# Four heads by 32 keys in a score tile, value rows through a DRAM tensor, and halved first projections, in a two-layer attention kernel

## The chip, the cores and the metric

The kernel runs on one core of a Trainium2 chip. The metric is the device time of one execution in microseconds (us), as the median of several runs. A profile of one execution gives the rest. The engines are TensorE (PE, with PEld for its weight loads), VectorE (DVE), ScalarE (ACT), GpSimd (POOL) and SyncE (SP); each works through its own queue in order. In this kernel SP computes nothing: it issues nearly all of the DMAs, the DMA transposes among them.

## What is computed

Four blocks follow each other on x (2048 tokens of 512 numbers): A, B, A, B, each added to x after a layer norm. Both have 32 heads of 16 dimensions. A is causal softmax attention inside four segments of 512 tokens, mixed by a gate with a linear-attention memory of the earlier segments. B is linear attention over all tokens, with softmax feature maps. The gate g depends on the head alone.

```python
# A, per segment s of 512 tokens (the rest of the head's state is M and z)
logits = einsum('bhqd,bhkd->bhqk', qs, ks) * scale + mask      # causal
a_dot  = einsum('bhqk,bhkd->bhqd', softmax(logits), vs)
a_mem  = (phi(qs) @ M) / (phi(qs) @ z + 1e-06)
o      = g * a_mem + (1 - g) * a_dot
M, z   = M + phi(ks).T @ vs,  z + sum(phi(ks))
...
# B
phi_q, phi_k = [softmax(p), softmax(-p)] of q @ w_phi and k @ w_phi
o = (phi_q @ (phi_k.T @ v)) / (phi_q @ sum(phi_k) + 1e-06)
```

## The kernel before

**Order.** The program is first recorded as a graph of operations, with the tiles that they read, write and open. Then `place` (L157) reads a packed table, `ORDER`: it gives the place of each operation in one sequence, its engine where there is a choice (an eviction of a PSUM tile can go to ACT or to DVE), and the buffer of each tile. Nothing is planned at run time: each engine works off its operations in the table's order and waits on semaphores for what an operation needs. An operation that waits holds up all behind it on its engine, on SP too. Pools hold the buffers: four PSUM tiles of 128x1024 (`pD`), three buffers of masked keys (`pQ`, class KM), 22 general buffers of 1024 columns (`p2`, where the exponentials PT lie), two of values (`pV`, VT), two of swapped values (`pW`, VS), two of PE and three of PF for the exponentials at the diagonal. (The class PE, tile `pE`, is not the engine PE.)

**Projections.** `a_proj` (L695) makes keys, queries and values of a segment. For each pair of head groups (a group is 8 heads, 128 rows) K and Q come out of TensorE with tokens along the columns (`KQ`, matmuls of 64 rows and 512 columns, two row halves side by side, `pair` at L330), are evicted to `KT` and `QT`, and `kmask` (L666) spreads the keys: four DVE instructions per pair multiply KT by a column mask, so that in KM a block of 128 columns holds 64 keys of one head beside 64 keys of another, with zeros in the rows of the other heads. In the first segment K and Q of one group share one PSUM tile, so that a tile waits for all 512 tokens.

**Scores.** `a_att` (L819) treats two query tiles of 128 at once (256 queries, `i0` is 0 or 2) for each of four groups g. A score tile in PSUM is 128 rows (two heads by 64 keys) by 1024 columns (two row halves, two blocks of 64 keys, 256 queries). For key tiles ahead of the diagonal (`j < i0`) all of it is needed: label S, four tiles in a group when i0 is 2, none when it is 0, one ACT exponential of 1024 columns each. At the diagonal a group has three tiles: two of 896 columns (label Sf, exponential to `pF`) and one of 768 (label Sd, to `pE`): the causal edge is cut in steps of 64 queries. The triangle itself is added in PSUM by two matmuls of a tile, of a constant (`two64`) with the mask `tri`.

**Values.** The exponentials are the weights of the PV matmuls (label PV, `pvmm` at L871), 64 rows (64 keys of one head) by 128 queries; 17 value columns (16 and a one that sums the row) are the moving side, written twice, the second time to columns nobody reads, so that a matmul has 34 columns. Values are evicted to VT with tokens as rows. A head whose exponentials lie in the other half of the rows needs its values there too: two DMAs of a segment (`vsw`, L760, both from SP) copy half of VT to VS with the row halves swapped, inside SBUF. Half of the PV matmuls read VT, half VS.

Per segment follow the memory products, the output projection, a layer norm and B's keys (`b_keys`); after four segments B's queries (`b_query`), and then layer two. Where the text says (L, s), it means layer L, segment s, from 0.

## Time and profile before

| what | value |
|---|---|
| time, median of 3 runs | 466.94 us (466.38 to 467.51) |
| profiled execution, span from the first to the last instruction | 466.4 us |
| mean granted TensorE clock | 0.996 |
| instructions | 25392 |

The runs' time holds some half a microsecond that lies outside the profiled span (466.94 against 466.4). The page gives for each engine its busy time, the time per 40th of the span, the chain of work that ended last (followed back from the last instruction, each step to what released it), and groups of instructions by source line, engine and operation, with the mean time of one. In a group, "xcount | busy, mean" are the count, the union of their times in us and the mean of one in ns. Two things to know: many operations are recorded through helpers, so L351 is any ACT instruction, L326 and L341 any matmul, L360 a DVE eviction; and an ACT or PE instruction's time holds some 0.1 us and more of pipeline beyond the moment at which the next one starts, so that the time from one start to the next, as the chain shows it, is the smaller and is what a queue pays.

### The profile page before, as it was taken

Reading aid. Unit: us, or ns where it says so; the run is one execution under the profiler, and the core shown is the slowest. Engines: PE = TensorE matmul, PEld = TensorE weight load, DVE = VectorE, ACT = ScalarE, POOL = GpSimd, SP = SyncE. Lnnn points to the kernel's source line nnn. Section 1 sums busy time; section 2 is a strip of 40 time slices with the busy share of each in tenths; the row PEclk is TensorE's granted clock in tenths of the full one; section 3 lists DMA queues with packets and bytes.
Section 4 is the critical chain, followed back from the end, with each engine's and each line's share of the span. In section 5 each row is a group of like instructions: output and inputs, shape, how many; then the busy total and the mean of one; then the engine's idle time right before and its main releaser. Section 6 shows DMA issues by size and latency. Waiting matters only on the chain.

```text
span 466.4 us, 25392 instructions
## 1 busy us (share of the span) xinstructions
PE 444.9 (95%) x11765; PEld 296.2 (64%) x11765; DVE 410.1 (88%) x761; ACT 426.3 (91%) x556; POOL 55.6 (12%) x139
## 2 busy tenths in 40 slices
PE   8999999899999999998899999999999999999897
PEld 4457566666766686655546677566767676667554
DVE  5998889799779978986899999899988896999897
ACT  5899999899999999688999999999999999877992
POOL 2433011010011001100311221010100020110000
PEclk9999999999999999998999999999999999999999
DMA  8965653703212121200134564441233004110255
GB/s 260 191 132 123 87 88 57 74 5 71 51 26 49 21 42 28 38 7 4 32 62 84 77 96 75 70 73 37 47 41 59 17 15 60 27 25 1 38 94 181
DMA packets 87755, 29.96 MB, mean 64 GB/s; under 512 B 74322, under 2 KB 87650, under 8 KB 87650
## 3 DMA queue, kind: packets, MB, share of 16 engines
q1 hardware_dynamic: 86818, 27.81, 33.7%
q8 instruction: 92, 1.51, 1.4%
q10 hardware_dynamic: 800, 0.52, 0.4%
q0 software_dynamic: 32, 0.02, 0.2%
q14 instruction: 13, 0.11, 0.1%
HBM read 6.31 MB, written 2.10 MB: 18 GB/s over the span
## 4 chain that ended last, share of the span: by engine, by line
PE 59%; ACT 30%; DVE 6%; DMA 2%; POOL 1%; issue 1%; DVEq 0%; ACTq 0%
PE D L341 38%; PE D L326 18%; ACT p L351 16%; ACT pF L351 9%; ACT pE L351 4%; DMA pX<-p 2%; PE D L686 2%; DVE X L958 1%; ACT pS L351 1%; POOL rstd L599 1%; DVE stats L589 1%; DVE p L360 1%; DVE pV L360 1%; DVE p L815 1%; DVE p L610 0%
## 5 line engine op out<-in xcount | busy, mean ns | idle before, releaser
L351 ACT ACTIVATE p<-D 128x1024 bf16<-128x1024 f32 (+1 forms) x228 | 225.3, 1028 | 14.8 <-PE D L341 11.1
L326 PE MATMUL D<-pK,pQ 64*128 64x256 bf16 (+3 forms) x1536 | 114.4, 243 | 5.3 <-ACT p L351 1.2
L351 ACT ACTIVATE pF<-D 128x896 bf16<-128x896 f32 x128 | 116.4, 940 | 1.8 <-PE D L326 1.3
L326 PEld LDWEIGHTS D<-pK,pQ 64*128 64x128 bf16 x1536 | 54.4, 94 | 41.3 <-ACT p L351 6.0
L326 PE MATMUL D<-pV,pF 64*128 64x34 bf16 x1024 | 76.0, 176 | 1.3 <-issue 0.6
L326 PE MATMUL D<-pW,pF 64*128 64x34 bf16 x1024 | 73.4, 176 | 0.0
L326 PEld LDWEIGHTS D<-pV,pF 64*128 64x128 bf16 x1024 | 56.0, 93 | 3.9 <-ACT pF L351 1.2
L597 POOL TENSOR_SCALAR rstd<-mv 128x1 f32<-128x1 f32 x60 | 16.8, 286 | 346.6 <-DVE mv L590 346.0
L351 ACT ACTIVATE pE<-D 128x768 bf16<-128x768 f32 x64 | 52.5, 826 | 2.9 <-PE D L326 2.5
L326 PEld LDWEIGHTS D<-pW,pF 64*128 64x128 bf16 x1024 | 52.8, 93 | 1.9 <-issue 0.6
L326 PE MATMUL D<-pV,p 64*128 64x34 bf16 x1024 | 53.3, 176 | 0.0
L326 PE MATMUL D<-pW,p 64*128 64x34 bf16 x1024 | 52.3, 176 | 0.0
L326 PEld LDWEIGHTS D<-pV,p 64*128 64x128 bf16 x1024 | 47.4, 93 | 3.3 <-ACT p L351 0.6
L326 PEld LDWEIGHTS D<-pW,p 64*128 64x128 bf16 x1024 | 46.1, 93 | 1.9
L326 PE MATMUL D<-tri,two 64*128 64x128 bf16 (+1 forms) x384 | 46.3, 234 | 0.0
L589 DVE BATCH_NORM_STATS2 stats<-X 128x6 f32<-128x512 bf16 x63 | 42.0, 679 | 3.9 <-DMA X<-in_A_x_dram 3.5
L326 PE MATMUL D<-pV,pE 64*128 64x34 bf16 x512 | 45.4, 175 | 0.1
L326 PE MATMUL D<-pW,pE 64*128 64x34 bf16 x512 | 43.4, 175 | 0.0
L958 DVE TENSOR_TENSOR X<-X,D 128x1024 bf16<-128x1024 bf16 (+1 forms) x36 | 39.1, 1097 | 4.5 <-PE D L341 4.0
L1005 DVE TENSOR_REDUCE pS<-p 128x64 f32<-128x1024 bf16 (+1 forms) x36 | 38.6, 1091 | 2.7 <-ACT p L351 2.7
L341 PE MATMUL D<-pX,WA_k 64*128 64x512 bf16 x256 | 37.0, 377 | 0.1
L341 PE MATMUL D<-pX,WA_q 64*128 64x512 bf16 x256 | 36.9, 377 | 0.1
(127 smaller groups left out, 966.2 us busy)
## 6 DMA issues: line engine op xcount, KB each, us to landing
pW<-pV SPq DMA_DIRECT2D x16, 136.0 KB, 3.3
out_dram<-X SPq DMA_DIRECT2D x7, 256.0 KB, 2.4
X<-in_A_x_dram SPq DMA_DIRECT2D x3, 512.0 KB, 6.7
pX<-in_B_wqkv_dram SPq DMA_DIRECT2D x3, 512.0 KB, 5.2
p<-p SPq DMA_TRANSPOSE x73, 3.1
pX<-p SPq DMA_TRANSPOSE x54, 3.2
WA_k<-in_A_wk_dram SPq DMA_DIRECT2D x2, 256.0 KB, 6.8
WB_o<-in_B_wo_dram SPq DMA_DIRECT2D x8, 64.0 KB, 2.9
```

The source lines that it names most:

```text
L326: ins = e.matmul(out_ap, lhsT, rhs, start=st, stop=sp, tile_position=(basep(lhsT), basep(out_ap)))
L341: ins = e.matmul(out_ap, lhsT[64 * hf:64 * hf + 64], rhs[64 * hf:64 * hf + 64], start=k == 0 and i == 0, stop=k == 1 and i == len(lists[hf ...
L351: return self.g.op({"act": (dur, lambda e: e.activation(out_ap(), in_ap(), func, scale=scale))}, reads, writes, opens, label=label)
L360: "dve": ((340 if fast else n / 0.96 + 65), lambda e: e.tensor_copy(out_ap(), in_ap()))}
L589: v(lambda e: e.bn_stats(self.stats[:, t, :], self.X[:, t, :]), 602, [R("X", t)], [R("st", t)], label="bn")
L597: v(lambda e: e.tensor_scalar(rs, self.mv[:, t, 1:2], LN_EPS, None, op0=ALU.add), 170, [R("mv", t)], [R("rstd", t)], eng="pool", label="rstd")
L599: v(lambda e: e.tensor_tensor(rs, rs, self.mhalf[:], ALU.pow), 540, [R("rstd", t), R("mhalf")], [R("rstd", t)], eng="pool", label="rstd")
L686: ins = e.matmul(D.t[c0:, r0 * 8:r0 * 8 + n], r[:, c0:], ones(r, n), start=True, stop=True, tile_position=(r0, c0))
L815: v(lambda e: e.tensor_tensor(tmp.t[:].rearrange("p (y h r d) -> p y h r d", y=16, h=2, r=2), NM.t[:, :].rearrange("p (h y r d) -> p y h r ...
L958: self.v(lambda e: e.tensor_tensor(X(), X(), src(), ALU.add), 65 + 512 * n / 0.96, pr + xr, xr, label="res")
L1005: fn = lambda e, sgn=sgn, eo=eo, Z=Z, n=n: e.tensor_reduce(Z.t[:, 0:64 * n].rearrange("p (k s h) -> p k s h", k=n, s=2)[:, :, sgn, :], eo( ...
```

## The change

- A score tile holds four heads by 32 keys. `kmask` writes runs of 32 keys where it wrote 64. Count, size and rows of the full tiles (S) stay.
- The diagonal of two query tiles is cut in steps of 32 queries. A group still has three tiles and three exponentials, now of 896, 768 and 640 columns (classes PP, buffers `pP1` to `pP3`), in place of 896, 896 and 768. Their matmuls are other ones, listed in `diagonal`.
- A PV matmul's 64 rows are two heads by 32 keys. Its moving side is a block of 34 columns, 17 of each head, with zeros where row and column belong to different heads. All PV matmuls read VS. The count is as before.
- VS is made through a DRAM tensor, `v_rows`: for each half of a segment (two token tiles) one DMA stores VT there (`vst`) and four DMAs (`vsw`) fetch 32 rows' worth each, in rows of 136 numbers, to the quarter of the partitions and the column half where they belong. The zeros are written once, at the start. VT and VS are now half a segment each; there are two buffers of VT and three of VS.
- The first segment's K and Q are projected in halves of 256 tokens for both groups of a pair, and the keys masked by halves. The load of token tiles 2 and 3 is recorded later.
- `p2` has 19 buffers in place of 22.
- A new table: all operations are placed anew.

```diff
-        self.pQ = pool("pQ", N_KM, [128, 8, 2, 2, 128], BF16, {}, ("KM",))
+        self.pQ = pool("pQ", N_KM, [128, 8, 4, 4, 32], BF16, {}, ("KM",))
+        self.scr = nc.dram_tensor("v_rows", [2, NSEG, 2, 2, 128, 544], BF16)
...
+        self.pV = pool("pV", N_V, [128, 2, 4, 8, 17], BF16, {}, ("VT",))
+        self.pW = pool("pW", N_VS, [128, 2, 2, 4, 8, 17], BF16, {}, ("VS",))
+        self.pP = {x: pool(f"pP{x}", n, [128, 4, 256], BF16, {}, ("PP",)) for x, n in zip((1, 2, 3), N_P)}
...
+        for i, tp in enumerate(self.pW.tensors):
+            self.pW.init[i] = two(lambda e, tp=tp: e.memset(tp[:], 0.0), 1900.0, 700.0)
...
+            out = lambda sl=sl: (... KM.t[:].rearrange("p j x a k -> p (j x) a k")[:, :, sl, :])
+            src = lambda: (... KT.t[:].rearrange("p (x k) -> p x k", k=32))
...
             if first:
-                for k, g in enumerate(gs):
+                for h in range(2):
                     ps = self.T(self.pD, "gen")
-                    self.wproj(ps, (self.WA["k"], self.WA["q"]), wk + wq, (g, g), xT, opens=[KT, QT, pk] if k == 0 else [], label="KQ")
+                    self.pair(lambda ps=ps, h=h, gs=gs: [[(ps.t[:, b * 512 + k * 256:b * 512 + k * 256 + 256], W[:, dt, g * 128:(g + 1) * 128], xT.t[:, dt, h * 256:(h + 1) * 256])
+                                                          for dt in range(4) for k, g in enumerate(gs)] for b, W in enumerate((self.WA["k"], self.WA["q"]))],
+                              [256] * 8, [xT[2 * h], xT[2 * h + 1]] + wk + wq, [ps[0], ps[512]], opens=[KT, QT, pk] if h == 0 else [], label="KQ")
...
+            self.dma(lambda V=V, D=D, t2=t2: [(D[t2 // 2].rearrange("t p c -> p t c"), V.t[:].rearrange("p t a k c -> p t (a k c)"))], 1,
+                     [V], [R("VD", L, s, t2)], lat=1900.0, label="vst")
+            for a in range(4):
+                self.dma(lambda W=W, D=D, t2=t2, a=a: [(W.t[32 * a:32 * a + 32, a % 2].rearrange("m t x k c -> m (t x) (k c)"),
+                                                         D[t2 // 2].rearrange("t (x m) (a c) -> m (t x) a c", x=4, a=4)[:, :, a])], 1,
+                         [R("VD", L, s, t2)], [W[a]], lat=1900.0, label="vsw")
...
+    def diagonal(x):
+
+        lead = [(0, 32 * x, 256 - 32 * x, 0, x, 32 * x), (1, 32 * x, 128 - 32 * x, 1, x, 128 + 32 * x)]
+        return {1: lead + [(1, 128, 128, 0, 0, 128)], 2: lead + [(1, 128, 128, 0, 3, 128)],
+                3: [(0, 96, 32, 0, 3, 96), (0, 128, 128, 0, 0, 0), (1, 96, 32, 1, 3, 224), (1, 128, 128, 1, 0, 128)]}[x]
...
+                for x in (1, 2, 3):
+                    self.mm(lambda S=S, x=x, key=key, qry=qry: [
+                        (S.t[:, hf * 512 + 256 * r + c:hf * 512 + 256 * r + c + n], key(hf, i0 + j, k), qry(hf, q, n), u == 0, False)
+                        for u, (r, c, n, j, k, q) in enumerate(self.diagonal(x)) for hf in range(2)] + [
+                        (S.t[:, hf * 512:hf * 512 + 512].rearrange("p (a b) -> p a b", a=2)[:, :, 32 * x:32 * x + (64 if x == 3 else 32)], one4(hf), tri(hf, 4 if x == 3 else 2), False, True)
+                        for hf in range(2)], [], rd(i0) + trir, [S], opens=[P], label="Sd", rows=64, dur={1: 223, 2: 197, 3: 219}[x])
+                    self.act(lambda P=P, x=x: P.t[:, :, 32 * x:256], lambda S=S, x=x: S.t[:, :].rearrange("p (a b) -> p a b", a=4)[:, :, 32 * x:256],
+                             ACT.Exp, 4 * (256 - 32 * x), [S], [P], scale=0.25, label="expd")
...
-N_XT, N_KM, N_K1, N_K2, N_VT, N_SM, N_QT, N_PE, N_PF = 5, 3, 10, 22, 5, 6, 3, 2, 3
-PVW = 320
+N_XT, N_KM, N_K1, N_K2, N_VT, N_SM, N_QT, N_V, N_VS = 5, 3, 10, 19, 5, 6, 3, 2, 3
+N_P = 2, 2, 2
```

Three places of the new order, word for word, a row for an instruction or several equal ones (line, operation, output from input, size). On PE, the first group of scores in the first segment. D is PSUM, pK and pQ are queries and masked keys, WA_v the weights of the values. Before, the three diagonal tiles with a value projection between them:

```order
L326 MATMUL D<-pK,pQ 128x256 x2
L326 MATMUL D<-pK,pQ 128x192 x2
L326 MATMUL D<-tri,two 128x2x64 x2
L341 MATMUL D<-WA_v,pX 128x512 x8
L326 MATMUL D<-pK,pQ 128x128 x2
L326 MATMUL D<-pK,pQ 128x64 x2
L326 MATMUL D<-pK,pQ 128x128 x2
L326 MATMUL D<-pK,pQ 128x64 x2
L326 MATMUL D<-tri,two 128x2x128 x2
```

Now, one tile of 192, 64 and 128 columns, and a value projection of eight matmuls ahead of the first full tile:

```order
L326 MATMUL D<-pK,pQ 128x192 x2
L326 MATMUL D<-pK,pQ 128x64 x2
L326 MATMUL D<-pK,pQ 128x128 x2
L326 MATMUL D<-tri,rep 128x2x32 x2
L341 MATMUL D<-WA_v,pX 128x512 x8
L326 MATMUL D<-pK,pQ 128x256 x4
L341 MATMUL D<-WA_v,pX 128x512 x8
L326 MATMUL D<-pK,pQ 128x256 x4
```

The matmuls of the diagonal tiles are narrower; the first projection of the values stands behind one diagonal tile, as before.

On SP, around the values of the last segment (1, 3). A transpose from p to pX feeds a projection, one from p to p the memory or an output projection. Before, the last three swaps of the program:

```order
L760 DMA pW<-pV 64x4x272
L364 DMA_TRANSPOSE p<-p 128x4x128 x4
L760 DMA pW<-pV 64x4x272
L364 DMA_TRANSPOSE p<-p 128x4x128
L760 DMA pW<-pV 64x4x272
L364 DMA_TRANSPOSE pX<-p 128x4x128 x2
```

Now, both stores and all eight fetches of that segment in one block, which nothing divides:

```order
L364 DMA_TRANSPOSE p<-p 128x4x128 x4
L368 DMA v_rows<-pV 128x2x544 x2
L368 DMA pW<-v_rows 32x8x136 x8
L364 DMA_TRANSPOSE p<-p 128x4x128
L364 DMA_TRANSPOSE pX<-p 128x4x128 x2
```

The swaps stood apart among transposes and needed evicted values alone; the fetches stand behind a store whose landing the first of them waits for, and the transposes behind wait with it.

On SP in the first segment, before and now, from the first transposes of the second segment's tokens on (pX from pX are weights that are folded):

```order
L364 DMA_TRANSPOSE pX<-p 128x4x128 x2
L462 DMA pX<-in_B_wqkv_dram 128x4x512
L364 DMA_TRANSPOSE pX<-pX 128x4x128
L760 DMA pW<-pV 64x4x272 x2
L364 DMA_TRANSPOSE pX<-pX 128x4x128 x5
```

```order
L368 DMA v_rows<-pV 128x2x544
L364 DMA_TRANSPOSE pX<-p 128x4x128 x2
L368 DMA pW<-v_rows 32x8x136 x2
L364 DMA_TRANSPOSE pX<-pX 128x4x128
L368 DMA pW<-v_rows 32x8x136 x2
L368 DMA v_rows<-pV 128x2x544
L368 DMA pW<-v_rows 32x8x136 x4
```

Two issues stood there, behind the second eviction of values; now ten, of which the first half of the segment's five stand around two token transposes and a weight transpose.

More of the change, by code (lines that the diff above doesn't have):

```diff
@@ L409, in alloc @@
         self.eps6 = sb("eps6", [128, 1], F32)
[L410 to L412 removed]
+        self.rep4 = sb("rep4", [128, 4, 32], BF16)
+        self.tri = sb("tri", [128, 32], BF16)
+        self.scr = nc.dram_tensor("v_rows", [2, NSEG, 2, 2, 128, 544], BF16)
         self.ones8 = sb("ones8", [128, 8], F32)
@@ L475, in setup @@
         ldx(0, 2, "act")
-        ldx(2, 2)
         for h in range(2):
@@ L660, in phi @@
         cut = lambda t: t.t[:, c0:c0 + n]
-        D, S, E = ([t[k] for k in keys] for t in (dst, src, e_))
+        D, E = ([t[k] for k in keys] for t in (dst, e_))
+        S = [src[(k, h)] for k in keys for h in range(2)]
         self.act(lambda: cut(e_), lambda: cut(src), ACT.Exp, n, S, E, psum=False, label="phexp")
@@ L673, in kmask @@
                 ch["act"] = (93 + n / 1.2, lambda e, sl=sl, out=out: e.activation(out(), src(), ACT.Copy, scale=self.m4[:, sl:sl + 1]))
-            self.g.op(ch, [KT[k] for k in keys] + [self.R("m4")], [KM[(k, sl)] for k in keys], label="Km", port=True)
+            self.g.op(ch, [KT[(k, h)] for k in range(2) for h in halves] + [self.R("m4")], [KM[(sl, h)] for h in halves], label="Km", port=True)
     def warm(self):
@@ new lines, in a_att @@
+                        P = PT[(y, j)] = self.T(self.p2, "PT")
+                        self.mm(lambda S=S, j=j, y=y, key=key, qry=qry: [(S.t[:, hf * 512 + z * 256:hf * 512 + z * 256 + 256], key(hf, j, 2 * y + z), qry(hf, 0, 256), True, True)
+                                                                         for z in range(2) for hf in range(2)], [], rd(j), [S], opens=[P], label="S", rows=64, dur=222)
+                        self.act(lambda P=P: P.t[:], lambda S=S: S.t[:], ACT.Exp, 1024, [S], [P], scale=0.25, label="exp")
@@ L1141, in build @@
                 self.loads[self.late].deps.add(gate)
-                for o in list(self.pV.init.values()) + list(self.pE.init.values()) + list(self.pF.init.values()):
+                for o in [o for p in (self.pV, self.pW, *self.pP.values()) for o in p.init.values()]:
                     o.deps.add(gate)
```

297 lines of the change are left out of this document (130 added, 167 removed).

## The prediction

> **What bounds the kernel now.** I read the page first, then the busy time by stage, then the chain of waits, then the groups by form. The page's busy times and its chain:
>
> ```profile
> span 466.4 us, 25392 instructions
> ...
> PE 444.9 (95%) x11765; PEld 296.2 (64%) x11765; DVE 410.1 (88%) x761; ACT 426.3 (91%) x556; POOL 55.6 (12%) x139
> ...
> PE 59%; ACT 30%; DVE 6%; DMA 2%; POOL 1%; issue 1%; DVEq 0%; ACTq 0%
> PE D L341 38%; PE D L326 18%; ACT p L351 16%; ACT pF L351 9%; ACT pE L351 4%; DMA pX<-p 2%; PE D L686 2%; DVE X L958 1%; ACT pS L351 1%; POOL rstd L599 1%; DVE stats L589 1%; DVE p L360 1%; DVE pV L360 1%; DVE p L815 1%; DVE p L610 0%
> ```
>
> Two engines share the end, PE with 59% of the chain and ACT with 30%; L341 is projections, L326 scores and PV, the ACT rows exponentials. A busy PE is pipelined, so I don't read its 95% as its load; the chain says it better. By stage (columns: stretch, its length, busy us and count of PE, PEld, DVE, ACT, POOL, granted clock, DMA share, GB/s):
>
> ```profile
> 24.00:56.00 32.00, 29.74 (x870) 20.53 (x866) 29.76 (x69) 32.00 (x40) 7.38 (x13) 1.00 0.60 116
> 140.00:172.00 32.00, 30.72 (x1016) 22.76 (x1014) 30.33 (x48) 31.90 (x41) 3.59 (x8) 1.00 0.19 35
> 344.00:374.00 30.00, 29.83 (x934) 21.33 (x928) 25.95 (x43) 29.39 (x35) 1.68 (x4) 1.00 0.17 30
> 410.00:420.00 10.00, 10.00 (x134) 6.14 (x130) 9.78 (x14) 7.89 (x9) 1.43 (x4) 1.00 0.12 18
> ```
>
> In the attention stages ACT has no idle time to speak of (32.00 of 32.00), and PE little; only in B's stretches (410 to 420) is ACT slack. What attention gains must therefore be gained on both. The clock is full, so it decides nothing here.
>
> **The diagonal's exponentials.** 64 groups (2 layers, 4 segments, 2 values of i0, 4 head groups) have three each, of 896, 896 and 768 columns, now 896, 768 and 640: 256 columns less.
>
> ```profile
> L351 ACT ACTIVATE p<-D 128x1024 bf16<-128x1024 f32 x220 | 220.7, 1043 | 12.0 <-PE D L341 8.5 <-PE D L326 2.5
> L351 ACT ACTIVATE pF<-D 128x896 bf16<-128x896 f32 x128 | 116.4, 940 | 1.8 <-PE D L326 1.3
> ...
> L351 ACT ACTIVATE pE<-D 128x768 bf16<-128x768 f32 x64 | 52.5, 826 | 2.9 <-PE D L326 2.5
> ```
>
> From 1024 to 768 columns the mean falls by 217 ns, whether the columns lie in two runs or four. 64 x 217 ns = 13.9 us less on ACT. The new order gives some back, by moving evictions from DVE: counted over the whole order, ACT does one more of 1024 columns, three more of 512 and one of 272.
>
> ```profile
> L359 ACT ACTIVATE p<-D 128x512 bf16<-128x512 f32 x11 | 6.6, 601 | 7.0 <-PE D L926 4.6 <-PE D L341 2.4
> ```
>
> At 1.04, 0.60 and (an estimate) 0.3 us that is 3.1 us: ACT falls by 10.8. DVE loses about as much and gains a zeroing and two sums for `rep4`; I count DVE at nothing.
>
> **The diagonal's matmuls.** Columns per group and row half, before: twice 256 + 192 + 128 for the triangle, and 128 + 64 + 128 + 64 + 256: 1792. Now 224 + 96 + 128 + 64, then 192 + 64 + 128 + 64, then 32 + 128 + 32 + 128 + 128: 1408. The two row halves run side by side. The price of a pair comes from the chain (eight matmuls of 512 columns) and from a stretch of nothing but PV matmuls of 34 (PE's busy us and count, clock, DMA):
>
> ```profile
> 17.99 0.86 PE D L341 x8
> ```
>
> ```profile
> 302.40:303.20 0.80, 0.80 (x70) 1.00 0.00 0
> ```
>
> 0.86 us / 4 pairs / 512 = 0.42 ns a column, so 384 columns are 161 ns. But 35 pairs of 34 columns took 0.80 us, 23 ns each, not the 14 of their columns: a narrow pair has a floor. The two pairs of 32 columns in a group cost 10 ns more each than by columns. 161 - 20 = 141 ns, x 64 = 9.0 us less on PE. The 5120 PV matmuls keep count, rows and 34 columns: nothing. Full tiles keep everything.
>
> **How the two combine.** The chain passes through both. Its exponentials at the diagonal (13% of 466.4, 61 us) shrink as 217 does to 2706 (940 + 940 + 826): 4.9 us. Its L326 (18%, 84 us) shrinks as the 141 ns do to a group's mean of some 2.2 us for scores and PV (0.75 at the diagonal by 0.42 ns a column, 0.43 for two full tiles on average, 0.92 for 80 PV matmuls): 5.4 us. Together 10.3. If only the exponentials' part came through: 4.9. I take 9.0, the smaller of the two engines' savings, since neither can run ahead of the other for long with four PSUM tiles.
>
> **The start.** ACT's timeline, the last bracket being idle time and its cause:
>
> ```profile
> 9.51 1.56 ACT L359 ACTIVATE pX<-D 128x512 bf16<-128x512 bf16 x3
> 13.50 0.60 ACT L359 ACTIVATE p<-D 128x512 bf16<-128x512 f32 x1 [2.43 <-PE D L341]
> ...
> 16.09 1.03 ACT L351 ACTIVATE p<-D 128x1024 bf16<-128x1024 f32 x1
> ```
>
> ACT waits 2.43 us for the first K, which waits for four token tiles and 16 matmuls of 512 columns (1.72 us by the row above). Halved, they take 0.86 and need two tiles. At most the 2.43 goes, at least nothing, since a masking of keys on ACT now stands ahead of the first exponential in place of behind it. I take 1.5 us less. The load of X that is recorded later keeps its place as SP's first.
>
> **The value rows.** The swap's landing, stores to DRAM and SP's issues:
>
> ```profile
> pW<-pV SPq DMA_DIRECT2D x16, 136.0 KB, 3.3
> out_dram<-X SPq DMA_DIRECT2D x7, 256.0 KB, 2.4
> ```
>
> ```profile
> 23.74 1.33 SPq L760 DMA_DIRECT2D pW<-pV  x2
> 25.79 6.09 SPq L364 DMA_TRANSPOSE pX<-pX  x4
> ```
>
> ```profile
> L326 PE MATMUL D<-pW,pF x1024: 175/175/189, 29.5 to 403.9; 64*128 64x34 bf16 x171
> ...
> L360 DVE CAST pV<-D x13: 1189/1226/1227, 21.7 to 334.3; 128x1024 bf16<-128x1024 f32 x13
> ```
>
> Before, from an evicted V to a landed VS: one issue ahead (0.67) and 3.3, 4.0 us; the first PV at 29.5 came 1 to 2 us behind the landing of the second swap. Now: a store of 272 KB (2.4 by the DRAM row, 3.3 by the SBUF one), three issues (2.0) ahead of the last fetch, and its 3.3: 7.7 to 8.6 us, in the first segment 1.5 more for the weight transpose between. So 5.2 to 6.1 us later there, less what the eviction comes earlier: only half a segment is awaited, and some four us of DVE's work that stood ahead of that eviction now stand behind it (counted from the order, by the groups' means). That leaves 1.2 to 2.1, of which ACT, with 1.6 us more of exponentials placed ahead of the first PV, hides most or nothing. In (1, 3) store and fetches stand directly ahead of their readers: 1.2 for the eviction and 8.6, against nine to eleven us of matmuls that PE has between: nothing to 1. Elsewhere five to nineteen us of exponentials lie between the fetches' issue and the first reader, which hides them. Zeroing three VS buffers goes to POOL (12% busy) and DVE. I take +1.5 for all, between 0 and +5; if the cover is gone everywhere it is the rival below.
>
> The Trainium skill ("DMA: Bandwidth & Descriptors", Specifications) states that runs under 512 bytes don't reach line rate, since they are read, changed and written. The fetches' runs are 136 numbers, 272 bytes, where the swaps' were 544; it speaks against the change. By it a fetch of half the swap's bytes would take as long as the swap, so the sum stays; without it a few tenths less. The same page ("Anatomy of one DMA") puts most of a DMA's some 2 us on the receipt of its last write, heaviest for DRAM; the 2.4 above agrees, but was taken in the quiet end of the program.
>
> **Masking keys** in runs of 32:
>
> ```profile
> L671 DVE TENSOR_SCALAR pQ<-p,m 128x1024 bf16<-128x1024 bf16 x56 | 25.4, 472 | 0.1
> L610 DVE TENSOR_SCALAR p<-X,mv,rstd 128x512 bf16<-128x512 bf16 x63 | 24.5, 401 | 2.1 <-ACT rstd L595 1.2 <-POOL rstd L599 0.5
> ...
> L671 DVE TENSOR_SCALAR pQ<-p,m 128x512 bf16<-128x512 bf16 x14 | 4.4, 336 | 0.0
> ```
>
> No row shows runs of 32. Lower bound: as runs of 64, nothing. Upper: the column's price (136 ns / 512 = 0.27 ns) doubles: 56 x 272 + 14 x 136 ns = 17 us on DVE. I take nothing: the same operation on unbroken rows, with two column operands (L610), costs 401 ns where runs of 64 with one cost 336, so runs of 64 cost nothing that shows, and 32 is nearer to 64 than to no packing at all.
>
> **Sum.** 466.4 - 9.0 - 1.5 + 1.5 = 457.4, and with the half us between span and median (466.94) 457.9: **458 us**. Its own range: best 10.3 + 2.4 off and nothing on, 454; worst 4.9 off and 5 on, 467.
>
> **Rivals.** *SP is held (slower).* A segment has ten issues and two waits for a store's landing on SP, where it had two issues: (10 - 2) x 0.67 + 2 x 2.4 to 3.3 = 10 to 12 us more of SP per segment. Behind stand the token transposes, on which projections wait. Where such a transpose is late, all is:
>
> ```profile
> 82.14 5.46 DMA pX<-p
> ...
> 172.08 3.94 DMA pX<-p
> ```
>
> ```profile
> SPq L364 <- DVE p L610: 36.7, 12, 12.0
> ```
>
> Against it: SP mostly waits for DVE, as in this row, and so has time. It decides from 9 / 8 = 1.1 us per segment on the path; at 2 us per segment it is 458 + 16 = 474. *DVE takes over:* with 17 us more it is busy 427 of 458; half on the path gives 466, no change. *ACT's part alone comes through:* 466.9 - 4.9 - 1.5 + 1.5 = 462. *Buffers:* 19 in place of 22 in `p2` and half a segment less of VS make exponentials wait; one of 0.91 us in each of the 16 half segments gives 458 + 14 = 472. The time by stage shows ACT full with 22, which speaks neither way.
>
> **How the numbers follow.** Forecast 0.60; ACT alone 0.14; SP held 0.15; DVE 0.06; buffers 0.05. What a measurement can tell from no change is 0.2%, 0.9 us. Faster: 0.60 + 0.14, and a third of DVE's 0.06, less 0.02 for the forecast's upper edge: 0.74. Slower: 0.15 + 0.05 + 0.01 = 0.21; same 0.05. The range, 452 to 470, takes in the forecast's and reaches to the nearer half of the slower cases.
>
> **What would show it.** Diagonal exponentials of 940, 826 and about 715 ns; ACT near 416 us busy; the first exponential by 14.6; the first PV by 31; masking at 472 ns; no wait of PE for fetches over 2 us. Wrong if the chain shows DMA over 4%, fetched VS or pX<-p among its first rows, or DVE over 420.

## The result: slower by 0.6%, and the profile after

| | before | changed |
|---|---|---|
| time, median of 20 runs each | 467.53 us | 469.37 us (467.33 to 473.69) |
| profiled execution, span | 466.4 us | 469.9 us |
| granted TensorE clock, mean | 0.996 (runs beside the experiments) | 0.986 (the 20 runs) |

The ratio is 1.0058 with a 95% interval of 1.0037 to 1.0079: slower, where 458 us was forecast. The range (452 to 470) holds the time. In the experiments below an execution more than 1.5% above the fastest of its kernel is left out of the ratio, though not of the median. The page's span, busy times and chain of the changed kernel:

```profile
span 469.9 us, 26174 instructions
...
PE 441.6 (94%) x12085; PEld 296.9 (63%) x12085; DVE 414.0 (88%) x761; ACT 420.2 (89%) x561; POOL 58.6 (12%) x140
...
PE 58%; ACT 21%; DVE 13%; issue 3%; DMA 3%; POOL 1%; DVEq 0%; SPq 0%
PE D L341 37%; PE D L326 19%; ACT p L351 13%; ACT pP L351 8%; DMA pX<-p 2%; PE D L696 2%; DVE X L955 1%; DVE stats L594 1%; DVE pQ L681 1%; DVE p L360 1%; DVE p L615 1%; ACT pS L351 1%; DVE p L1108 1%; DMA pW<-v_rows 1%; DVE pV L360 1%
```

PE's and ACT's busy time has shrunk (444.9 to 441.6, 426.3 to 420.2, which is less than the 9.0 and 10.8 that were forecast), DVE's has grown (410.1 to 414.0), and so has the whole: what was saved is lost to waits and to the clock. In the chain ACT went from 30% to 21%, DVE from 6% to 13%, "issue", which is time in which nothing visible is waited for, from 1% to 3%. The groups by form show that the parts themselves cost what the prediction said, the exponentials (940, 826, 715 expected) and the masking (472):

```profile
L351 ACT ACTIVATE pP<-D 128x896 bf16<-128x896 f32 x64 | 59.1, 931 | 3.3 <-DVE pP L555 1.6 <-PE D L326 1.3
L351 ACT ACTIVATE pP<-D 128x768 bf16<-128x768 f32 x64 | 51.7, 818 | 3.6 <-PE D L326 3.2
L351 ACT ACTIVATE pP<-D 128x640 bf16<-128x640 f32 x64 | 45.2, 717 | 1.7 <-PE D L326 1.1
...
L681 DVE TENSOR_SCALAR pQ<-p,m 128x1024 bf16<-128x1024 bf16 x56 | 25.5, 471 | 0.1
```

Store and fetch of the value rows land about as fast as taken (2.4 to 3.3 and 3.3 in the prediction), by the page's DMA issues:

```profile
v_rows<-pV SPq DMA_DIRECT2D x16, 272.0 KB, 3.4
pW<-v_rows SPq DMA_DIRECT2D x64, 68.0 KB, 3.1
```

So the durations of the instructions were right. What they are worth, and what stands around them, was not.

### The profile page after: what moved, and what is told of

It reads as the page before. It is cut to its first block, busy times and chain, and to the rows that moved or that the text cites. A ratio compares the mean times of both kernels' runs of the same rounds, so it can differ in the third digit from the quotient of the medians.

```text
span 469.9 us, 26174 instructions
## 1 busy us (share of the span) xinstructions
PE 441.6 (94%) x12085; PEld 296.9 (63%) x12085; DVE 414.0 (88%) x761; ACT 420.2 (89%) x561; POOL 58.6 (12%) x140
## 4 chain that ended last, share of the span: by engine, by line
PE 58%; ACT 21%; DVE 13%; issue 3%; DMA 3%; POOL 1%; DVEq 0%; SPq 0%
PE D L341 37%; PE D L326 19%; ACT p L351 13%; ACT pP L351 8%; DMA pX<-p 2%; PE D L696 2%; DVE X L955 1%; DVE stats L594 1%; DVE pQ L681 1%; DVE p L360 1%; DVE p L615 1%; ACT pS L351 1%; DVE p L1108 1%; DMA pW<-v_rows 1%; DVE pV L360 1%
## 5 line engine op out<-in xcount | busy, mean ns | idle before, releaser
L351 ACT ACTIVATE pP<-D 128x768 bf16<-128x768 f32 (+2 forms) x192 | 148.7, 822 | 8.6 <-PE D L326 5.6
L326 PE MATMUL D<-pK,pQ 64*128 64x256 bf16 (+6 forms) x1792 | 112.2, 228 | 5.1 <-ACT pP L351 1.3
L326 PE MATMUL D<-pW,pP 64*128 64x34 bf16 x3072 | 84.4, 175 | 3.3 <-issue 2.7
L326 PEld LDWEIGHTS D<-pW,pP 64*128 64x128 bf16 x3072 | 69.5, 93 | 10.2 <-issue 4.1
L326 PE MATMUL D<-tri,rep 64*128 64x64 bf16 (+1 forms) x384 | 39.6, 197 | 0.0
L341 PE MATMUL D<-pX,WA_q 64*128 64x512 bf16 (+1 forms) x288 | 38.4, 360 | 0.3 <-issue 0.2
L341 PE MATMUL D<-pX,WA_k 64*128 64x512 bf16 (+1 forms) x288 | 37.0, 353 | 0.8 <-DVE pV L360 0.8
L341 PE MATMUL D<-pX,WB_q 64*128 64x512 bf16 x256 | 35.2, 400 | 1.1 <-DVE pS L1082 0.9
L604 POOL TENSOR_TENSOR rstd<-rstd,mhalf 128x1 f32<-128x1 f32 x60 | 35.2, 595 | 3.1
L341 PE MATMUL D<-WB_k,pX 64*128 64x512 bf16 (+1 forms) x288 | 33.8, 353 | 1.3 <-DMA pX<-p 1.2
```

Of the source, the lines that this page charges most:

```text
L326: ins = e.matmul(out_ap, lhsT, rhs, start=st, stop=sp, tile_position=(basep(lhsT), basep(out_ap)))
L341: ins = e.matmul(out_ap, lhsT[64 * hf:64 * hf + 64], rhs[64 * hf:64 * hf + 64], start=k == 0 and i == 0, stop=k == 1 and i == len(lists[hf ...
L351: return self.g.op({"act": (dur, lambda e: e.activation(out_ap(), in_ap(), func, scale=scale))}, reads, writes, opens, label=label)
L604: v(lambda e: e.tensor_tensor(rs, rs, self.mhalf[:], ALU.pow), 540, [R("rstd", t), R("mhalf")], [R("rstd", t)], eng="pool", label="rstd")
```

## The experiments

Each kernel was timed beside runs of the kernel before on the same chip; a ratio is to those. Where a difference from the changed kernel is given, it is (ratio - 1.0058) x 467.5 us, with the two intervals combined, some 1.6 us either way.

### The zeroing of the three VS buffers, moved to the start

The first place to look was DVE in the first segment. DVE's timeline of the changed kernel (start, duration, instruction), of which these rows matter:

```profile
13.50 0.33 DVE L681 TENSOR_SCALAR pQ<-p,m 128x512 bf16<-128x512 bf16 x1
...
14.62 0.41 DVE L615 TENSOR_SCALAR p<-X,mv,rstd 128x512 bf16<-128x512 bf16 x1
...
15.20 0.69 DVE L594 BATCH_NORM_STATS2 stats<-X 128x6 f32<-128x512 bf16 x1
15.80 1.63 DVE L615 TENSOR_SCALAR p<-X,mv,rstd 128x512 bf16<-128x512 bf16 x1
...
18.69 2.10 DVE L681 TENSOR_SCALAR pQ<-p,m 128x512 bf16<-128x512 bf16 x1
...
44.17 1.87 DVE L552 MEMSET pW<- 128x2176 bf16 x1 [0.40 <-issue]
```

and POOL's beside it:

```profile
15.38 1.91 POOL L552 MEMSET pW<- 128x2176 bf16 x1
...
18.71 1.93 POOL L552 MEMSET pW<- 128x2176 bf16 x1
```

An instruction of 0.41 us takes 1.63 and ends just behind POOL's memset (17.43 and 17.29); one of 0.33 takes 2.10 and ends likewise (20.79 and 20.64). The chain of waits has both in it, and the third memset, which stands on DVE itself. The zeroing was counted at nothing because POOL has time; but while POOL writes these, the two DVE instructions stand. The Trainium skill ("SBUF — State Buffer", SBUF: two separate sides) states that GpSimd shares a pair of ports with VectorE's instructions of certain modes as an exclusive lock, and that the loser blocks for the other's whole instruction. The two rows agree; which mode a DVE instruction ran in, no row shows.

The run moves all three to the start, onto POOL, and writes the zeros in words of four bytes (half as many elements):

```diff
-        self.pW = pool("pW", N_VS, [128, 2, 2, 4, 8, 17], BF16, {}, ("VS",))
+        self.VS4 = [sb(f"pW{i}", [128, 1088], F32) for i in range(N_VS)]
+        self.pW = Pool("pW", [t[:, :].bitcast(BF16).rearrange("p (a b c d e) -> p a b c d e", a=2, b=2, c=4, d=8) for t in self.VS4])
...
-            self.pW.init[i] = two(lambda e, tp=tp: e.memset(tp[:], 0.0), 1900.0, 700.0)
+            self.pW.init[i] = two(lambda e, i=i: e.memset(self.VS4[i][:], 0.0), 1900.0, 700.0)
...
+        spot = next(o for o in order if o.eng == "pool" and o.label == "one" and o not in early)
+        order = [o for o in order if o not in early]
+        k = order.index(spot)
+        order[k:k] = early
```

> The change with one thing moved: the three VS buffers are zeroed on POOL between 2 and 7 us, where POOL and DVE wait for the first load, and in 4-byte words. Theory Z (the zeroing holds DVE: in the profile of the change two of DVE's instructions, 1.63 and 2.10 us long instead of 0.41 and 0.33, end with POOL's two zeroings of 1.9 us, and a third zeroing stands on DVE itself for 1.87 us, all three in the chain): 3.0 + 1.9 us come off DVE before 47 us, and 3 to 5 us off the whole, so 464.5 to 466.5. Theory V (the rows' way over DRAM is what was lost) and theory K (PE's clock and its instruction fetch): within 1 us of the change, 468.4 to 470.4.

Measured: 467.45 us, ratio 0.9986 (0.9958 to 1.0015), 3.4 us under the changed kernel (1.8 to 5.1). The three zeroings now run at 2 us, and the two DVE instructions are back at 0.40 and 0.34 (timelines of POOL and DVE):

```profile
2.02 2.89 POOL L561 MEMSET pW<- 128x1088 f32 x3
```

```profile
16.13 0.40 DVE L624 TENSOR_SCALAR p<-X,mv,rstd 128x512 bf16<-128x512 bf16 x1
...
17.78 0.34 DVE L690 TENSOR_SCALAR pQ<-p,m 128x512 bf16<-128x512 bf16 x1
```

The rows account for it: 1.22 and 1.77 us of blocking and a memset of 1.87 us on DVE, 4.9 in all, of which 3.4 came off the whole. The zeroing, which the sum had at 0, costs about 3.

### The value rows, fetched without waiting for the store

The fetches take rows of the input in place of `v_rows`, and wait for no store; the PV products are then of other numbers.

```diff
-                                                         D[t2 // 2].rearrange("t (x m) (a c) -> m (t x) a c", x=4, a=4)[:, :, a])], 1,
-                         [R("VD", L, s, t2)], [W[a]], lat=1900.0, label="vsw")
+                                                         self.inp["A_x"][0][t2 * 128:t2 * 128 + 256].rearrange("(t x m) c -> m (t x) c", t=2, x=4)[:, :, 120 * a:120 * a + 136])], 1,
+                         [], [W[a]], lat=1900.0, label="vsw")
```

> The change, but the 64 fetches of value rows read as many bytes of the input in DRAM and wait for no store, so the values are wrong; stores, issues and traffic stay. Theory V: SP's waits for the stores' landing (11.3 us in the profile) and PE's for VS go, 3 to 5 us less than the change, 464.5 to 466.5. Theories Z and K: the stores' landing is hidden nearly everywhere, so at most 1 us less, 468.4 to 469.4.

Measured: 469.04 us, 1.0027 (1.0001 to 1.0053), 1.4 us under the changed kernel by the ratios (3.0 under to 0.1 over) and 0.3 by the medians. With the zeroing early as well:

> The early zeroing and fetches that read the input and wait for no store (wrong values), together. With the zeroing gone the profile shows PE waiting 0.9 us for fetched rows at 30 us, before the first PV. If the rows' way over DRAM was hidden by the zeroing alone: 1 to 3 us under the early zeroing's 467.45, so 464.5 to 466.5. If its cover is other work: within 0.7 us of it, 466.8 to 468.2.

466.34 us, 0.9985 (0.9951 to 1.0018): no better than the early zeroing alone, give or take 2 us. So the waits for the store cost 0 to 1.5 us, with an uncertainty as large, and the +1.5 of the sum fits. Of the rival in which SP is held, some 16 us, these runs take away the waits for the store's landing; the ten issues of a segment stay. That rival works by late token transposes, and PE's waits for them (us in all, times, the longest) are the same before and in the changed kernel:

```profile
PE D L341 <- DMA pX<-p: 1.2, 2, 1.0
```

```profile
PE D L341 <- DMA pX<-p: 1.2, 2, 0.9
```

So it shows neither in the runs nor in the trace.

### The diagonal, undone here and put into the kernel before

First the changed kernel with its diagonal tiles as wide as before:

```diff
-        lead = [(0, 32 * x, 256 - 32 * x, 0, x, 32 * x), (1, 32 * x, 128 - 32 * x, 1, x, 128 + 32 * x)]
+        y = 1 if x < 3 else 2
+        lead = [(0, 32 * y, 256 - 32 * y, 0, x, 32 * y), (1, 32 * y, 128 - 32 * y, 1, x, 128 + 32 * y)]
...
-                    self.act(lambda P=P, x=x: P.t[:, :, 32 * x:256], ...
+                    self.act(lambda P=P, y=(1, 1, 2)[x - 1]: P.t[:, :, 32 * y:256], ...
```

> The change with the diagonal's columns as they were (exponentials 896, 896 and 768, matmuls 1792 columns a group; more of the triangle is computed than is used, and the output is wrong). If the diagonal's 9 us did come through in the change and something else of 10 us took them, 9 us more than the change: 478. If they never came through there, under 3 us more: below 472.4.

476.79 us, 1.0197 (1.0164 to 1.0229): 6.5 us over the changed kernel. Then the kernel before, in its own order, with exponentials of 896, 768 and 640 columns and 384 columns less for PE in a group. It leaves out some scores at the causal edge.

```diff
-                                (S.t[:, hf * 512 + 64:hf * 512 + 448].rearrange("p (b c) -> p b c", b=2)[:, :, 0:64], two(hf), tri(hf, 2), False, True) ...
+                                (S.t[:, hf * 512 + 128:hf * 512 + 512].rearrange("p (b c) -> p b c", b=2)[:, :, 0:32], two(hf), tri(hf, 2)[:, :, 0:32], False, True) ...
...
-                    self.act(lambda P=P: P.t[:, :, 64:512], lambda S=S: S.t[:].rearrange("p (a b) -> p a b", a=2)[:, :, 64:512], ...
+                    self.act(lambda P=P, p=p: P.t[:, :, 64 + 64 * p:512], lambda S=S, p=p: S.t[:].rearrange("p (a b) -> p a b", a=2)[:, :, 64 + 64 * p:512], ...
```

> The kernel before, with the diagonal's exponentials cut to 896, 768 and 640 columns and its matmuls to the change's 1408 columns a group (two pairs fewer than the change has); the cut columns are left out, so the output is wrong. It asks what the diagonal is worth by itself. By the prediction's term: 9.0 us less than before, 458.5; with both engines' terms on the chain 10.3, 457; if only the exponentials' part of the chain counts 4.9, 462.6. If the diagonal gains nothing to speak of because PE's clock is gated for each us that PE idles more: over 464.

462.75 us, 0.9912 (0.9877 to 0.9947): 4.1 us under before, from 2.5 to 5.8. Its page:

```profile
PE 435.9 (95%) x11765; PEld 289.4 (63%) x11765; DVE 408.8 (89%) x761; ACT 415.5 (90%) x556; POOL 56.0 (12%) x139
...
PE 65%; DVE 17%; ACT 11%; DMA 3%; issue 2%; POOL 1%; DVEq 0%
```

PE lost 9.0 us of busy time, the prediction's figure, and ACT 10.8; the time lost half of the 9.0. The chain suggests where the rest went: ACT fell from 30% to 11%, and DVE, whose work is the same, rose from 6% to 17%. No run made DVE's work smaller in this kernel, so that DVE is what holds it is read from the chain and not shown. The two halves alone, the exponentials (their diff is the second pair above) and, of the matmuls, those that add the triangle, at half their columns (256 of the 384; it leaves parts of the triangle out):

> The kernel before with the diagonal's exponentials alone cut to 896, 768 and 640 columns (13.9 us less on ACT); PE computes all columns as before, and the cut ones are left out of the result. By the prediction's rule, that the smaller of the two engines' savings comes through: 0, so 467.2. By the chain's share, where the exponentials count as far as they stand in it: 4.9 us, 462.5, and then the narrowing of both (measured 5.05 less) is nearly all ACT's.

> The kernel before with the diagonal's masking matmuls alone cut from 512 to 256 columns a group (256 of the 384 columns that the change saves, 107 ns x 64 = 6.9 us on PE); the exponentials stay, and the triangle is masked only in part. By the rule of the smaller saving: 0, so 467.2. By the chain's share of PE in scores and PV: two thirds of 5.4, 3.6 us less, 463.6. If PE's load alone sets the pace: 6.9 less, 460.3.

The exponentials alone gave 0.9946 (0.9924 to 0.9968), 2.5 us; the matmuls alone 0.9991 (0.9969 to 1.0013), nothing that can be told. The chains of the first and of the second:

```profile
PE 69%; ACT 18%; DVE 8%; DMA 2%; issue 1%; POOL 1%; DVEq 0%; SPq 0%; ACTq 0%
```

```profile
PE 52%; ACT 34%; DVE 7%; DMA 3%; issue 1%; POOL 1%; DVEq 0%
```

Shorten one engine's work, and the other's share of the chain grows (30% and 59% before). Still, neither "the smaller saving" (0 for one engine alone) nor the shares of the chain (4.9 for the exponentials; 3.6 for 256 of the 384 columns whose share was 5.4) gives these numbers: ACT's saving pays half its share, PE's nothing alone that can be told.

### The start, undone

K and Q of the first pair wait for four token tiles again:

```diff
-                              [256] * 8, [xT[2 * h], xT[2 * h + 1]] + wk + wq, ...
+                              [256] * 8, [xT[t] for t in range(2 * h if gp or h else 0, 2 * h + 2 if gp or h else 4)] + wk + wq, ...
...
-        self.g.place(self.pools, ORDER)
+        self.g.place(self.pools, ORDER, (), ((124, 125),))
```

> The change with its first half projection held back until all four token tiles are there, as before (0.9 to 1.3 us later on PE). If the earlier start was worth something in the change (the prediction's 1.5 us): 0.9 to 1.5 us slower than the change, 470.3 to 470.9. If DVE, which stands in the chain from 12 to 35 us, made it worthless: within 0.4 us, 469 to 469.8.

474.36 us, 1.0136 (1.0112 to 1.016): 3.6 over the changed kernel. The first exponential comes at 16.4 us in place of 15.0, but that is not all: PE then waits for an eviction of values,

```profile
22.47 0.37 PE L352 MATMUL D<-pX,WA_k 64*128 64x256 bf16 x1 [2.89 <-DVE pV L371]
```

and from 22.4 us the clock is halved for 3.41 us. In this order the halved projection is worth 3.6 us (2.2 to 5.1), at least the 1.5 of the sum, but part of that is the wait and the clock window that its loss brings.

### A load in the way of instructions

PE's timeline of the changed kernel has a hole of 2.11 us "<-issue" (the first two rows); SP's row under it is a load of 512 KB, issued 4.5 us ahead of the hole.

```profile
62.20 0.17 PE L326 MATMUL D<-pW,pP 64*128 64x34 bf16 x1
64.48 0.19 PE L326 MATMUL D<-pW,pP 64*128 64x34 bf16 x1 [2.11 <-issue]
```

```profile
57.68 0.58 SPq L461 DMA_DIRECT2D pX<-in_B_wqkv_dram  x1
```

The queues from 56.1 to 62.0 us and from 62.0 to 64.5:

```profile
q1 hardware_dynamic: 1965, 0.91, 63.0%
```

```profile
q1 hardware_dynamic: 1119, 0.28, 137.6%
q8 instruction: 1, 0.02, 2.3%
```

q8 brings instructions, 95 packets of 16 KB in the execution. While the load runs none comes; one begins at 62.1, takes 0.92 us, and PE goes on some 1.4 us after its end. Here this load stands 102 places later in the order, ahead of a later token transpose, and the transpose of the folded weights that needs it is moved too:

```diff
-        self.g.place(self.pools, ORDER)
+        self.g.place(self.pools, ORDER, (), ((19, 375), (220, 813)))
```

> The change with one load moved on SP: the 512 KB of B's query weights, issued at 57.7 us just ahead of a run of PV matmuls, now go behind it (and the first transpose that reads them goes back too). Theory K (PE runs out of instructions at 62.2, since the 16 KB block of its next 256 instructions waits behind that load: the block's packet begins at 62.1, 7.5 us after the one before it, and PE goes on 1.4 us after it ends; the window of 3.4 us with that hole is followed by one at half clock): the 2.1 us hole and the window at 65 go, 2 to 4 us less than the change, 465.4 to 467.4. If the hole comes from PE's own pace through the PV matmuls, or the window from something else: within 1 us of the change.

467.82 us, 1.0015 (0.9988 to 1.0042): 2.0 us less (0.4 to 3.6). In its profile a packet of instructions begins at 60.3, in place of 62.1. PE's busy time and clock in two stretches, changed kernel first:

```profile
60.00:64.00 4.00, 2.37 (x101) 1.74 (x97) 3.90 (x8) 2.96 (x4) 0.50 (x2) 1.00 1.28 194
64.00:68.00 4.00, 3.52 (x112) 2.57 (x114) 1.86 (x5) 2.29 (x4) 0.28 (x1) 0.61 0.33 69
```

```profile
60.00:64.00 4.00, 3.81 (x189) 3.09 (x187) 3.93 (x8) 3.42 (x5) 0.35 (x2) 1.00 0.37 74
64.00:68.00 4.00, 3.98 (x81) 2.17 (x74) 3.71 (x9) 3.97 (x7) 2.05 (x6) 1.00 0.41 71
```

The hole is gone, and with it the halved clock (0.61) of the next 3.41 us. With the zeroing early, and a second load and a second weight transpose moved too, it missed:

> The change with early zeroing, the late 512 KB load, and two more rows moved on SP: the 512 KB load at 15.9 us and the weight transpose that stood between the first half segment's fetches go behind the fetches. If the causes add up: 469.4 - 1.9 - 1.6 - 0.9 (the wait for fetched rows at 30 us) = 465.0, faster than before by 0.5%. If only the largest counts: 466.5 to 467.5.

470.23 us, 1.0053 (1.0028 to 1.0079). A load that now stood late made PE wait 3.60 us for its transpose. Early zeroing with the late load alone, and the same with the weight transpose of the first half segment's fetches put behind them, ahead of the second store:

> The change with the early zeroing and the late 512 KB load of the query weights, and nothing else. If the zeroing (1.9 us alone) and the hole before the window at 65 us (1.6 alone) are separate causes, they add up: 465.9, faster than before by 0.3%. If they are one: 467.4.

> The same, and the weight transpose that stands between the first half segment's fetches goes behind them, so that the last two fetches are issued 1.2 us earlier. If PE's wait for them at 30 us (0.9) is all on the path: 465.0. If the fetches are then hidden by the next wait: 465.9, as without it. A loss would say that the transposes' place on SP matters more.

467.87 (1.0002, 0.9977 to 1.0026) and 467.47 (0.9996, 0.9972 to 1.0019): 2.6 and 2.9 under the changed kernel, no more than the zeroing alone. PE of the first shows why: with DVE's work earlier, the next thing is late at that place, a token transpose, and the clock is halved again at 64.9.

```profile
63.77 1.04 PE L352 MATMUL D<-pX,WA_q 64*128 64x512 bf16 x8 [2.52 <-DMA pX<-p]
```

The two gains don't add.

### The clock at the end

Half clock comes in windows of 3.41 us. The profile of before has one, from 218.0 us; that of the changed kernel has four, at 64.9, at 211.7 and two from 436.9. PE in the 3.4 us ahead of those two, by stretch and by form:

```profile
433.50:436.90 3.40, 2.71 (x179) 2.51 (x181) 2.36 (x6) 3.34 (x6) 0.00 (x0) 1.00 0.02 5
436.90:443.70 6.80, 5.26 (x124) 3.13 (x126) 6.03 (x15) 6.43 (x13) 0.00 (x0) 0.50 0.35 43
```

```profile
L326 PE MATMUL D<-Rz,p 64*128 64x8 bf16 x144 | 2.3, 163 | 1.0 <-DVE Rz L975 1.0
L326 PE MATMUL D<-Rkv,p 64*128 64x64 bf16 x35 | 1.1, 190 | 0.1
```

and at the same work before, where the clock stayed full:

```profile
429.60:433.00 3.40, 2.67 (x113) 1.74 (x109) 2.85 (x6) 3.10 (x5) 0.00 (x0) 1.00 0.00 0
```

```profile
L341 PE MATMUL D<-pX,WB_q 64*128 64x512 bf16 x9 | 1.4, 376 | 0.0
L326 PE MATMUL D<-Rz,p 64*128 64x8 bf16 x80 | 1.2, 163 | 0.7 <-DVE Rz L978 0.7
L341 PE MATMUL D<-pT,p 64*128 64x136 bf16 x12 | 0.7, 221 | 0.0
L326 PE MATMUL D<-Rkv,p 64*128 64x64 bf16 x12 | 0.3, 191 | 0.0
```

PE is equally busy (2.71 and 2.67 of 3.40). But the new order has put 179 narrow matmuls in a row, where before nine of 512 columns and twelve of 136 stood among them. Counting 2.4 columns per ns (0.42 ns a column, as in the prediction), with row halves side by side counted once, PE streamed columns for 0.21 of the one window and 0.47 of the other (0.22 and 0.39 if only matmuls that began inside count). By the latter count, over all windows at full clock of the 19 profiles, each of the 27 under 0.297 was followed by half clock, and none over 0.414; from 0.297 to 0.414, 15 were and 21 were not. By PE's busy share the two kinds overlap from 0.48 to 0.92, so the columns tell them apart better, though not fully. Nor is the new order alone in it: three profiles of the kernel before with parts of its diagonal narrowed have a halved window at this place too (at 427.9, 429.9 and 432.3 us).

Wide dummy matmuls, two of 256 columns at four places and one of 512 at three, were to clear it:

```diff
+                self.mm(lambda sgn=sgn, gp=gp: ([(ZQ.t[:, 256 + 512 * b:512 + 512 * b], self.ident[:], EQ[(gp, sgn)].t[:, 256 * b:256 * b + 256], True, True)
+                                                  for b in range(2)] if (L, c, gp, sgn) in FILL_Z else []) + ...
...
+FILL_Z = {(1, 0, 1, 0), (1, 2, 1, 1), (1, 2, 0, 0), (1, 1, 0, 1)}
```

> The change with 1.5 us of extra matmuls whose results are written over (seven times 512 columns, put into narrow operations of layer 1's last queries, at 429 to 438 us). Theory K: the clock's gate looks at how many columns PE streams in a window of 3.4 us, not at whether it is busy; the two windows at half clock there (6.8 us) come behind two with 0.22 and 0.16 of the columns that they could hold, and the extra ones lift these over 0.33, so the half windows go, and the kernel is 1 to 2.5 us faster than the change though it does more, 467 to 468.4, with a mean clock 0.004 to 0.008 higher. If the gate looks at idle time, or the half windows cost nothing since PE waits there anyway: 0 to 1.5 us slower, 469.4 to 471.

470.75 us, 1.0081 (1.0055 to 1.0107), 1.1 us over the changed kernel (0.5 under to 2.7 over): a miss, the profile has both windows still, from 438.4. The window ahead of them streamed 0.31 now, so the dummies were too few, or the columns don't decide. With the zeroing early and the load late too:

> The early zeroing, the late load and the extra matmuls together. If the three are separate causes, their gains add up: 1.9 (measured) + 3 + 1.7 = 6.6 us less than the change, 462.8, and so faster than before. If they share one cause or the saved time is lost to the next wait: 465 to 467.

467.3 us, 0.9982 (0.9947 to 1.0017). Its profile has no halved window there, behind a window that streamed 0.30: two windows with the same dummies and nearly the same columns (0.31, 0.30) and busy shares (0.89, 0.86) went two ways, so what sets the clock stays open. The end still took as long (38.2 us from the landmark of the table below). That doesn't acquit the clock, since this end holds some 1.5 us of extra matmuls. In the old order one halved window cost little: 36.0 us against 35.6 in the table. Then four of the narrow matmul groups, and what hangs on them, were put later in the order, behind the first wide projections of the last queries, in the changed kernel and in that with early zeroing:

```diff
-        self.g.place(self.pools, ORDER)
+        self.g.place(self.pools, ORDER, (), ((2754, 2725), (2755, 2725), (2753, 2725), (2756, 2725), (2757, 2725), (2758, 2725), (2759, 2725)))
```

> The change with four narrow PE operations near the end (and the three on ACT and DVE that use them) moved behind the first of the wide projections for the last 512 queries, so that the run of narrow matmuls at 429 to 437 us is broken up; nothing is added or taken away. If the two windows at half clock there (6.8 us) come from that run and lie on the path: one or both go, the mean clock rises by 0.004 to 0.007, and the kernel is 1 to 3 us faster than the change, 466.4 to 468.4. If they cost nothing, since PE waits for ACT there anyway: within 0.7 us of the change, 468.7 to 470.1.

> The same move at the end, in the change with the early zeroing (467.45 alone). If the clock's cost at the end is a cause of its own, the two add up: 464.5 to 466.5, faster than before by 0.2 to 0.6%. If not: 466.8 to 468.2.

475.91 us (1.0176, 1.0128 to 1.0224) and 473.47 us (1.0109, 1.007 to 1.0149): misses, 5.5 us over the changed kernel and 5.8 over the one with early zeroing. In the first, PE then waits 1.48 and 1.39 us for ACT and DVE, and a halved window comes at 447.7 in addition.

### All costs that were found, taken away at once

Early zeroing, the late load and fetches that wait for nothing (again with other numbers in the PV products); the diff is the sum of three above.

> The change with early zeroing, late load, and fetches that read the input and wait for no store (wrong values): all three found costs away at once. If with the diagonal's true worth (5 us in the order before) they close the account but for PE's clock: before's 467.5 - 5 + 1.2 to 2.9 for two more windows at half clock, so 463.7 to 465.4. Below 463: the clock costs nothing. Above 466: something large has not been found yet.

466.31 us, 0.9966 (0.9935 to 0.9997): 4.3 us under the changed kernel (2.5 to 6.0), and not the 7 that the three give alone. It lies over 466, so by the expectation something large has not been found. A landmark of the profiles, in us from the span's start:

| | before | changed | early zeroing | all taken away | before, narrow diagonal |
|---|---|---|---|---|---|
| end of the last exponential of B's query block (1, 0) | 430.8 | 431.4 | 427.7 | 423.7 | 423.6 |
| from there to the end | 35.6 | 38.5 | 38.2 | 39.1 | 36.0 |

With the costs away the changed kernel reaches this point when the kernel before with a narrow diagonal does, and behind it the variants of the new order need 2.6 to 3.5 us more than before. But they have more work behind it. These groups, from the landmark to the end, differ most, before and changed:

```profile
L341 PE MATMUL D<-pX,WB_q 64*128 64x512 bf16 x34 | 4.5, 377 | 0.0
L971 DVE TENSOR_TENSOR KV<-KV,D 128x544 f32<-128x544 f32 x1 | 0.7, 714 | 0.0
```

```profile
L341 PE MATMUL D<-pX,WB_q 64*128 64x512 bf16 x42 | 6.8, 446 | 0.1
L341 PE MATMUL D<-pT,p 64*128 64x136 bf16 x16 | 0.8, 220 | 0.0
L968 DVE TENSOR_TENSOR KV<-KV,D 128x544 f32<-128x544 f32 x3 | 2.1, 716 | 0.4 <-PE D L341 0.4
```

Eight matmuls of 512 columns and 16 of 136 are 1.3 us of PE by 0.42 ns a column and pair, and two sums 1.4 us of DVE, which the order of before has ahead of the landmark. So of the 2.9 us about half is work that was moved across it. The end itself is some 1.5 us longer, and the changed kernel loses some 1.3 us more ahead of the landmark than the table says.

## Why the prediction was wrong

The sum forecast 11.6 us less than the ratio gives (458 / 466.94 = 0.9809 against 1.0058, x 467.5).

**The step that failed** is the one that combined the two savings at the diagonal: "I take 9.0, the smaller of the two engines' savings, since neither can run ahead of the other for long with four PSUM tiles". Both savings were there in the narrowed kernel (9.0 and 10.8). But the smaller saving is not what comes through: ACT's alone, where the smaller is 0, gave 2.5 us, and both together 4.1. The argument names two engines, and three are 88% busy and more; the narrowed kernel's chain has DVE at 17% in place of 6%, which makes DVE the likely third bound, not shown by a run of its own. The term's value is 4.1 us in the order of before (2.5 to 5.8) and 6.5 in the new one (4.7 to 8.3); 9.0 is outside both. This term was too large by 2.5 to 4.9.

**"Zeroing three VS buffers goes to POOL (12% busy) and DVE"**, at nothing, named the idle time that was to hide it but not what it does to the neighbour: measured 3.4 us (1.8 to 5.1).

**"The clock is full, so it decides nothing here"** was read from before and applied to another order. There are now some four halved windows, by the mean of 20 runs (0.014 x 469.4 / 0.5 = 13 us, at 3.41 each), where before has one. Among the runs of one and the same kernel the time grows by 1.0 us for each halved window (0.8 to 1.1, over 304 runs of 19 kernels, from each run's mean clock), so 2.8 more go with some 2.7 us. How much of that they cost can't be separated from the waits that lead to them.

**The start** (-1.5) was right or too small: undoing it costs 3.6, though the first exponential came at 15.0, later than the 14.6 forecast. **The value rows** (+1.5) fit: 0 to 1.5, the first PV at 31.2 of 31, and no wait of PE for fetches over 1.0 us. **Masking** at nothing was right (471 ns). ACT's busy time fell by 6.1 of the 10.8 forecast, to 420 and not 416. None of the signs of being wrong came (DMA over 4%, fetched VS or `pX<-p` newly high in the chain, DVE over 420): they watched the rivals and not the term that failed.

What is left: of the 11.6, the diagonal's size takes 2.5 to 4.9. The costs found, away at once, give 4.3, of which 1.5 for the rows were in the sum: 2.8. The remaining 4 to 6 us, the longer end among them, stay open. Counted the other way they are more: without the diagonal (6.5) and the start (3.6) the new order would be some 12.8 us slower than before, if the two add, and 4.3 of that was found. Wide dummy matmuls, another order at the end and the two with early zeroing didn't shorten the end. Of the rivals, "SP is held" finds no support in the runs without a wait or in PE's waits for transposes, and "DVE takes over" falls by its mechanism (masking), though DVE's share of the chain doubled. *Buffers* finds no support in the trace: 9.8 us of the exponentials' waits in attention (5.0 before) were ended by the matmuls of their own scores, and none by a PV matmul, which is what frees a buffer of exponentials; a run with 22 was not made. The runs that were clearly faster than the kernel before leave out scores or take other numbers for the values.

## What to carry to other kernels

Where three engines are about 90% busy, a saving on two of them can be worth half of the smaller one, as here: try it in the old order, by narrowing the instructions, ahead of building anything on it. A cost that is "hidden on an idle engine" must also be looked at from that engine's neighbours, and a load also from the queue that carries instructions. And a new order brings its own waits and clock windows: the time of an order read from the old profile is no base for the new one.

## What the runs showed of the hardware

- A memset of 1.9 us on POOL held DVE's TENSOR_SCALAR until its end (1.63 and 2.10 us for 0.41 and 0.33), but not DVE's BATCH_NORM_STATS2, which ran beside the first memset, from 15.20, in 0.69 us as elsewhere.
- A load of 512 KB kept a 16 KB packet of instructions back, and PE stood 2.11 us with nothing to issue; with the load later, the packet came 1.8 us earlier and the hole was gone.
- The clock was halved behind windows in which PE was busy for 80% of the time and more (0.92 at most), with narrow matmuls. The Trainium skill ("TensorE: Matmul & The Clock Gate", Part 1: The HAM clock gate) states two clock rates and windows of 3413 ns, which the traces show (1.00 and 0.50, 3.41 us), and that the rate follows how busy PE was. Here the columns streamed told more than the busy time: 0.22 and 0.39 of a window at the same busy time of 2.7 us went two ways, but so did 0.31 and 0.30. What counts as busy stays open.
